# Attention values with the lower tile's keys first for all head pairs, as one accumulation per bank

## Chip, cores, metric

The kernel runs on one core of a Trainium2 chip. The metric is the device time of one execution in microseconds (us); times below are of that kind, or spans and stretches of one profiled execution. TensorE is called PE, its weight loads PEld, VectorE DVE, ScalarE ACT, GpSimd POOL, and SyncE, which issues nearly all transfers, SP.

## What is computed

Eight batches of eight heads, 576 positions, head width 64, all in float32. Attention is causal with a window of 128 keys and a linear bias by distance; its output, with the heads side by side, goes through a soft mixture of eight experts with four slots each.

```python
def _attn_ref(q, k, v):
    scores = scale * np.matmul(q, k.transpose(0, 1, 3, 2))
    ...
    mask = (rel >= 0) & (rel < window)          # window = 128
    scores = np.where(mask, scores + bias[None], -1000000000.0)
    ...
    return np.matmul(attn, v)

def _moe_ref(x, phi, w1, w2):                   # x: 4608 x 512
    logits = x @ phi                            # 32 slots
    ...                                         # d: softmax over tokens, c: softmax over slots
    slot_input = d.T @ x
    ...                                         # per expert: relu(slot_input @ w1) @ w2
    return c @ slot_out
```

## The kernel before

**Tiles and groups.** Each batch is cut into query tiles of 128 positions, t = 0 to 3, and a tail t = 4 of 64. Because the window is 128 keys, a query of tile t sees keys of its own tile up to itself, and keys of the lower tile t - 1 from itself on. A tile of t < 4 is worked in two groups, g = 0 and 1, of four heads each; a tail is one group of eight heads. There are 72 groups, and they pass through a software pipeline: the loop from line 773 on runs one group per step, and all engines execute their instructions in the order in which the program issues them.

**One step i of the loop.** DVE merges the scores of group i (`merge`, L279 to L283), takes row maxima (L301) and the bias (L304), and normalises the probabilities of group i - 1 (`normalise`, L317), with the reciprocal of a sum (L313) that POOL prepares (`total`, L309). PE turns the probabilities of group i - 3 (`flip`, L372) into the PSUM tile `pq`. ACT copies them to SBUF as `pa` (`split`, L379). Then PE computes the values of group i - 4 (`values`, L406), the scores of group i + 1 (L247, L252, L259, L266), and what else is due: `x_flip` (L434), `logits` (L452), `slot_sum` (L510). ACT ends the step with the four exponentials of group i (`expo`, L357); ahead of them it stores a finished query tile out of PSUM (`x_store`, L422) and keeps a flipped one (`x_keep`, L443). (For the first steps the lags are one less.)

**Two masked halves.** Scores of a group hold, in 128 columns, own-tile keys and lower-tile keys merged by a triangle, so the flipped probabilities must be split again. `split` does it on POOL with two triangular selects, in this order: L381 reads `pa` and writes the lower tile's part to another buffer, `pp`; L383 then masks `pa` in place for the own tile's part (`pd`). For a tail these are L386 and L388. For t = 0 there is no lower tile and no select.

**Values.** For head pair i of the group and for each half of the keys (`ph` 0: lower tile, from `pp`; `ph` 1: own tile, from `pd`), two matmuls with 64 columns of `v` as weights write 64 partitions each of the PSUM tile `xp`. One float32 matmul is two PE instructions (and two weight loads) in the profile. So a group with t of 1 to 3 has 2 pairs x 2 halves x 2 = 8 matmuls, 16 instructions; a tail 16 matmuls of 64 columns, 32 instructions; t = 0 has 4 matmuls. The order is pair by pair: lower, own, lower, own.

**Around it.** V tiles lie in three SBUF buffers; after the last group of a tile SP loads the next one (`load_v`, L191), and at the start of the last batch two tiles by halves (`load_v_pair`, L201). After the loop the last groups are unrolled by hand; there `split` and `values` of the last tail are cut in two (lines 812 to 835). From about 225 us on come the experts (L926, L963) and the combination (L988, L990).

Of the kernel before, what the change touches and what calls it, by code (L numbers as in the profile page):

```python
# [56 lines left out]
def width(t):  # L57
    return P if t < 4 else TAIL
# [10 lines left out]
def tile_attn_softmoe(  # L69
# [71 lines left out]
    st = {}  # L141
# [18 lines left out]
    number = {key: i for i, key in enumerate(groups)}  # L160
# [231 lines left out]
    def values(key, pairs=None, to=None):  # L392
        b, t, g = key
        w = width(t)
        if (b, t) not in st or to is not None:
            st[b, t] = ps_1.tile([P, NPAIR, P], F32, tag="xp", name="xp") if to is None else to
        xp = st[b, t]
        pd, pp = st[key]["pd"], st[key]["pp"]
        for i in pairs or range(2 if t < 4 else 4):
            j = 2 * g + i  # L400
            halves_of = (1,) if t == 0 else (0, 1)
            for ph in halves_of:
                for par in range(2):
                    h = 2 * j + par
                    src = pp if ph == 0 else pd
                    nc.tensor.matmul(  # L406
                        xp[D * par:D * par + D, j, 0:w], lhsT=v_slot[b, t - 1 + ph][:, D * h:D * h + D],
                        rhs=src[:, 2 * par + i] if t < 4 else src[:, 2 * par + i % 2, TAIL * (i // 2):TAIL * (i // 2) + TAIL],
                        start=(ph == halves_of[0]), stop=(ph == halves_of[-1]),
                    )  # L410

    def x_of(b, t):
# [357 lines left out]
    with tc.manual_schedule(engines=ORDERED):  # L770
        scores(0)
        loads(0)
        for i in range(n):
            new = groups[i]
            run("pre", i)
            if i:
                softmax_front(new, groups[i - 1])
            else:
                for us in (LO, HI):
                    merge(new, us)  # L780
                    rowmax(new, us)
                    bias(new, us)
                    expo(new, us)
            near = int(i < SKIP)
            if i + near >= FLAG and i != SKIP:
                flip(groups[i + near - FLAG])
                split(groups[i + near - FLAG])
            run("act", i)
            if i + near >= LAG and i != SKIP:
                values(groups[i + near - LAG])  # L790
                after_values(i, groups[i + near - LAG])
            if i + 1 < n:
                scores(i + 1)
            if i + 1 < n - 1:
                loads(i + 1)
            if i:
                expo(new)
            run("pe", i)
            load_weights_at(i)
            run("dve", i)  # L800
# [14 lines left out]
        slot_flip(end)  # L815
        token_max(end)
        values(ga)
        load_weight()
        load_weight()
# [7 lines left out]
        inverse(gd, LO)  # L827
        normalise(gd, LO)
        values(gb, range(0, 2), bank("xq"))
        flip(gd, LO, bank("pt"))  # L830
        split(gd, LO)
# [287 lines left out]
```

## Time and profile before

| | us |
|---|---|
| median of 3 runs | 291.06 (290.58 to 291.56) |
| the profiled execution's own time | 291.42 |
| its span, first to last instruction | 289.4 |

| engine | busy us | share of the span |
|---|---|---|
| PE | 256.3 | 89% |
| DVE | 222.4 | 77% |
| ACT | 206.2 | 71% |
| PEld | 179.0 | 62% |
| POOL | 112.3 | 39% |

The attention stage takes about the first 225 us of the span; experts and combination the rest. Between 25 and 200 us PE, DVE and ACT are each busy for some nine tenths of most stretches, so the shares over the whole span understate DVE and ACT there. "Idle before" in a row is the time that the engine stood still ahead of that instruction, with the instruction that ended the wait.

### The profile page before, as it was taken

The page shows a single profiled execution, that of the slowest core. Times are in us where ns is not written, and L with a number is a line of the kernel's source. Part 1 is how long each engine was busy: PE and PEld are TensorE (multiplying, and loading weights), DVE is VectorE, ACT ScalarE, POOL GpSimd, SP SyncE. Part 2 cuts the span into 40 slices and gives each one's busy share as a digit, 9 for nine tenths or more (in the row PEclk, how much of TensorE's full clock was granted, in tenths as well). Part 3 has the DMA queues.
Part 4 walks back from the last instruction along what each step waited for, and adds up shares of the span by engine and source line. Part 5 has one row for each costly group of instructions (what it writes and reads, how often), then busy time and mean ns, then how long its engine had stood idle before and what let it go on. Part 6 is the DMA issues. An engine that isn't in the chain of part 4 may idle for free.

```text
span 289.4 us, 13589 instructions
## 1 busy us (share of the span) xinstructions
PE 256.3 (89%) x5535; PEld 179.0 (62%) x5535; DVE 222.4 (77%) x509; ACT 206.2 (71%) x817; POOL 112.3 (39%) x218
## 2 busy tenths in 40 slices
PE   7598899789969989999998997998979989999990
PEld 3366666666657567766676764766666543587650
DVE  3889989898995989898898997799874344646442
ACT  2788888988885998997998898798784311044460
POOL 2044626662573267246617634466652012000000
PEclk9779999999998999999999999999999999999996
DMA  6646267868883998789678977877465579999897
GB/s 183 228 117 179 82 206 253 269 189 295 266 268 106 303 299 261 209 301 285 202 247 276 321 248 221 275 237 231 150 219 166 162 258 353 411 409 340 335 385 291
DMA packets 36754, 72.61 MB, mean 251 GB/s; under 512 B 4402, under 2 KB 15316, under 8 KB 36692
## 3 DMA queue, kind: packets, MB, share of 16 engines
q1 hardware_dynamic: 35972, 71.24, 74.5%
q8 instruction: 43, 0.70, 1.0%
q10 hardware_dynamic: 720, 0.51, 0.5%
q14 instruction: 19, 0.16, 0.2%
HBM read 62.29 MB, written 9.44 MB: 248 GB/s over the span
## 4 chain that ended last, share of the span: by engine, by line
PE 40%; ACT 18%; DVE 18%; POOL 13%; issue 6%; DMA 2%; DVEq 0%; ACTq 0%; POOLq 0%
ACT area L357 10%; PE xp L406 6%; PE op L963 5%; PE hp L926 5%; DVE area L317 5%; DVE s L301 4%; PE s L266 4%; POOL area L383 4%; POOL area L381 4%; PE po L988 3%; DVE s L281 3%; ACT area L379 3%; ACT area L422 2%; PE lp L452 2%; PE pq L372 2%
## 5 line engine op out<-in xcount | busy, mean ns | idle before, releaser
L357 ACT ACTIVATE area<-s,nb 128x128 f32<-128x128 f32 x286 | 103.1, 394 | 12.3 <-DVE nb L304 10.3
L406 PE MATMUL xp<-area 128*64 128x128 f32 (+1 forms) x1104 | 76.9, 274 | 12.1 <-POOL area L383 5.8
L406 PEld LDWEIGHTS xp<-area 128*64 128x64 f32 x1104 | 54.6, 138 | 23.3 <-POOL area L383 11.0
L357 ACT ACTIVATION_READ_ACCUMULATOR area<-s,nb 128x1 f32 x286 | 66.1, 231 | 0.0
L317 DVE TENSOR_TENSOR area<-area,rs 128x512 f32<-128x512 f32 (+1 forms) x73 | 61.6, 844 | 1.8
L379 ACT COPY area<-pq 128x512 f32<-128x512 f32 (+1 forms) x72 | 43.8, 610 | 14.5 <-PE pq L372 11.9
L301 DVE TENSOR_REDUCE s<-s 128x4 f32<-128x512 f32 x71 | 49.5, 697 | 2.2
L266 PE MATMUL s<-kq 64*32 64x160 f32 x1792 | 43.6, 306 | 1.1 <-issue 1.1
L383 POOL TENSOR_SCALAR_AFFINE_SELECT area<-area 128x512 f32<-128x512 f32 x48 | 42.4, 884 | 3.3
L309 POOL TENSOR_SCALAR rs<-sm 128x4 f32<-128x4 f32 x70 | 15.0, 214 | 73.9 <-ACT area L357 72.5
L381 POOL TENSOR_SCALAR_AFFINE_SELECT area<-area 128x512 f32<-128x512 f32 x48 | 34.5, 719 | 16.4 <-ACT area L379 14.8
L281 DVE COPY_PREDICATED s<-cst,s 128x512 f32<-128x512 int32 x48 | 33.1, 689 | 6.9 <-PE s L266 6.7
L372 PE MATMUL pq<-unit_r,area 64*128 64x64 f32 x552 | 31.4, 232 | 3.1 <-ACT area L322 2.6
L266 PEld LDWEIGHTS s<-kq 64*32 64x32 f32 x1792 | 30.1, 108 | 2.6 <-issue 1.9
L372 PEld LDWEIGHTS pq<-unit_r,area 64*128 64x128 f32 x552 | 23.4, 140 | 11.6 <-POOL rs L309 2.9
L259 PE MATMUL s<-ramp,ones 64*32 64x320 bf16 x448 | 18.9, 314 | 4.0 <-ACT area L357 3.6
L422 ACT COPY area<-xp 128x512 f32<-128x512 f32 (+1 forms) x37 | 21.2, 572 | 1.4 <-PE xp L406 0.8
L443 ACT COPY area<-pq 128x512 f32<-128x512 f32 x34 | 20.8, 612 | 0.3 <-PE pq L428 0.3
L434 PEld LDWEIGHTS pq<-unit_r,area 64*128 64x128 f32 x264 | 11.1, 140 | 13.0 <-issue 9.2
L990 ACT COPY ob<-po 128x512 f32<-128x512 f32 x19 | 10.4, 591 | 11.4 <-PE po L988 9.9
L313 DVE RECIPROCAL rs<-rs 128x4 f32<-128x4 f32 (+1 forms) x73 | 12.3, 169 | 5.1 <-POOL rs L309 4.4
L990 DVE COPY ob<-po 128x512 f32<-128x512 f32 x17 | 11.2, 687 | 6.6 <-PE po L988 5.8
(173 smaller groups left out, 329.8 us busy)
## 6 DMA issues: line engine op xcount, KB each, us to landing
w<-w SPq DMA_DIRECT2D x53, 512.0 KB, 5.5
out<-ob SPq DMA_DIRECT2D x36, 256.0 KB, 3.2
kq<-q_t SPq DMA_DIRECT2D x69, 128.0 KB, 3.4
kq<-k_t SPq DMA_DIRECT2D x32, 256.0 KB, 3.8
area<-v_n SPq DMA_DIRECT2D x31, 256.0 KB, 4.0
area<-w SPq DMA_DIRECT2D x8, 512.0 KB, 4.6
area<-v_n SPq DMA_DIRECT2D x12, 128.0 KB, 4.3
kq<-w SPq DMA_DIRECT2D x3, 512.0 KB, 6.0
```

Of the source, the lines that this page charges most:

```text
L266: nc.tensor.matmul(s4[32 * c:32 * c + 32, 2 * par + jj, 32 * r:32 * r + WIN], lhsT=qt[rows, 2 * h + jj if t == 4 else jj, 32 * r:32 * r + 32],
L281: nc.vector.copy_predicated(s4[:, :, P:2 * P], bc(mask_u, 1, 4), s4[:, :, 0:P])
L301: nc.vector.tensor_reduce(st[key]["mx"][:, us], merged(key, us), axis=AX.X, op=ALU.max, negate=True)
L317: nc.vector.tensor_tensor(p4, p4, bc(rs, 2, P), op=ALU.mult)
L357: nc.scalar.activation(s["p4"][:, u], merged(key, u), AF.Exp, bias=s["nb"][:, u:u + 1], scale=SCALE, accum_out=s["sm"][:, u:u + 1],)
L372: nc.tensor.transpose(s["pt"][:, u, r], s["p4"][rows, u], ident[rows, rows])
L379: nc.scalar.copy(pa[:, us].rearrange("p u (r w) -> p u r w", r=2), s["pt"][:, us])
L381: nc.gpsimd.affine_select(pp[:, us], pa[:, us], [[0, m], [-1, P]], ALU.is_gt, 0.0, base=0, channel_multiplier=1)
L383: nc.gpsimd.affine_select(pa[:, us], pa[:, us], [[0, m], [1, P]], ALU.is_ge, 0.0, base=0, channel_multiplier=-1)
L406: nc.tensor.matmul(xp[D * par:D * par + D, j, 0:w], lhsT=v_slot[b, t - 1 + ph][:, D * h:D * h + D], rhs=src[:, 2 * par + i] if t < 4 else ...
L422: eng.copy(dst, src[:, :, 0:w])
L990: copy_by[by](ob, po)
```

## The change

For each group the two loops change places: all head pairs take the lower tile's keys first (`ph` 0), then all take their own (`ph` 1). With t of 1 to 3 the 16 instructions of a group now read `pp` in the first 8 and `pd` in the last 8; in the order before, instructions 1 to 4 and 9 to 12 read `pp`, 5 to 8 and 13 to 16 `pd`. In a tail it is the first 16 of 32; before, the two took turns every 4. Since several pairs are now open in one PSUM bank at once, the start flag is set on the first matmul of each 64-partition half of the bank alone, for the whole query tile, and the stop flag on the last. The matmuls, their number and operands, and all other instructions are the same.

```diff
-        for i in pairs or range(2 if t < 4 else 4):
-            j = 2 * g + i
-            halves_of = (1,) if t == 0 else (0, 1)
-            for ph in halves_of:
+        parts = (1,) if t == 0 else (0, 1)
+        fresh = number[key] == 0 or st.get("bank", None) is not xp
+        st["bank"] = xp
+        done = (g == 1 or t == 4 or to is not None) and (pairs is None or pairs[-1] == 3)
+        inner = pairs or range(2 if t < 4 else 4)
+        for ph in parts:
+            for i in inner:
+                j = 2 * g + i
                 for par in range(2):
                     h = 2 * j + par
                     src = pp if ph == 0 else pd
                     nc.tensor.matmul(
                         xp[D * par:D * par + D, j, 0:w], lhsT=v_slot[b, t - 1 + ph][:, D * h:D * h + D],
                         rhs=src[:, 2 * par + i] if t < 4 else src[:, 2 * par + i % 2, TAIL * (i // 2):TAIL * (i // 2) + TAIL],
-                        start=(ph == halves_of[0]), stop=(ph == halves_of[-1]),
+                        start=(fresh and (ph, i) == (parts[0], inner[0])), stop=(done and (ph, i) == (parts[-1], inner[-1])),
                     )
```

## The prediction, made before the changed kernel ran

> **What bounds the kernel now.** I read four views: the stretches of the attention stage first, then the page's chain, the waits grouped by who ended them, and the timeline around one group; after that the chain in order of time.
>
> ```profile
> 25.00:200.00 175.00, 160.56 (x4023) 117.32 (x4025) 157.62 (x348) 152.80 (x639) 89.52 (x167) 0.99 0.77 243
> ```
>
> The columns are start and end, length, and the busy time of PE, PEld, DVE, ACT and POOL, then PE's clock. In these 175 us PE is busy 160.6, DVE 157.6, ACT 152.8: three engines at 92, 90 and 87%. No single one is the bound, and PE has 14.4 us of standing still that could be won at most here.
>
> ```profile
> span 289.4 us, 13589 instructions
> ...
> ACT area L357 10%; PE xp L406 6%; PE op L963 5%; PE hp L926 5%; DVE area L317 5%; DVE s L301 4%; PE s L266 4%; POOL area L383 4%; POOL area L381 4%; PE po L988 3%; DVE s L281 3%; ACT area L379 3%; ACT area L422 2%; PE lp L452 2%; PE pq L372 2%
> ```
>
> The chain that ended last runs through all four engines; the values (L406, 6%) and the two POOL selects that feed them (4% each) are on it.
>
> ```profile
> PEld xp L406 <- POOL area L383: 11.0, 22, 0.8
> PEld xp L406 <- POOL area L381: 5.5, 6, 1.3
> ACT area L379 <- PE pq L372: 11.9, 15, 3.0
> DVE s L281 <- PE s L266: 6.7, 12, 1.4
> SPq L191 <- PE xp L406: 35.9, 26, 4.5
> ```
>
> Columns: total us, times, longest. PE's weight loads stood still 22 times, 11.0 us together, for the second select. Downstream, ACT stood still 15 times for PE's flip and DVE 12 times for PE's scores: there a later PE is a later kernel.
>
> ```profile
> 103.60 0.97 POOL L383 TENSOR_SCALAR_AFFINE_SELECT area<-area 128x512 f32<-128x512 f32 x1
> 103.84 0.20 PEld L406 LDWEIGHTS xp<-area 128*64 128x64 f32 x4
> 104.62 0.63 PEld L406 LDWEIGHTS xp<-area 128*64 128x64 f32 x12 [0.59 <-POOL area L383]
> ...
> 37.53 0.90 PEld L406 LDWEIGHTS xp<-area 128*64 128x64 f32 x28 [0.50 <-POOL area L388]
> ...
> 63.96 0.90 PEld L406 LDWEIGHTS xp<-area 128*64 128x64 f32 x28 [0.21 <-POOL area L388]
> ```
>
> One such group: four instructions of lower-tile keys run at 103.84, PE stops for the select that ends at 104.57, and twelve are left behind it. In a tail 28 of 32 are left behind L388.
>
> **The change, part by part.** *The order.* After it, eight instructions stand ahead of the stop and eight behind it (a tail: 16 and 16). The stop's end is set by POOL and does not move; what moves is four instructions of 0.63/12 = 0.053 us, so 0.21 us, from behind the stop to ahead of it (a tail: 12 x 0.90/28 = 0.39 us). The mean stop, 11.0/22 = 0.50 us, exceeds 0.21, so four more fit in nearly always. Where PE does not stop, nothing changes. Over all 22 stops that is at most 4.6 us of PE's standing still; what counts is the part on the chain.
>
> *The flags.* Fewer start flags and the same instructions. A group of t = 0 overwrites throughout, one of t = 1 to 3 accumulates in half of its instructions:
>
> ```profile
> 61.33 0.85 PEld L406 LDWEIGHTS xp<-area 128*64 128x64 f32 x16
> ...
> 67.52 0.42 PEld L406 LDWEIGHTS xp<-area 128*64 128x64 f32 x8
> ```
>
> 0.053 us each in both, so I put overwriting against accumulating at 0, from both sides.
>
> *Waits and buffers.* No wait is added. Own-tile V is needed four instructions later, lower-tile V and `pp` come free four earlier. SP's 26 waits for a V buffer end up to 0.2 us sooner; the loads of q behind them wait for PE's scores in any case, so I count nothing, except for one place below. What hides it is the loads' lead over the values; if that were gone, it would show as a gain.
>
> *On the chain.* All pieces of it from 34 us on in which values follow a select or wait for V (the one ahead of them, at 29.5, frees only ACT's store of a tile, and I count 0):
>
> ```profile
> 34.84 0.90 PE xp L406 x12
> 37.54 1.04 PE xp L406 x28
> 46.21 0.88 PE xp L406 x12
> 63.96 1.03 PE xp L406 x28
> 85.59 1.28 PE xp L406 x12
> 107.84 0.88 PE xp L406 x12
> 112.51 0.88 PE xp L406 x12
> 133.29 0.88 PE xp L406 x12
> 153.54 0.88 PE xp L406 x12
> 167.18 0.68 PE xp L406 x8
> 179.99 0.88 PE xp L406 x12
> 189.00 0.88 PE xp L406 x12
> 197.00 0.69 PE xp L406 x13
> 202.33 0.88 PE xp L406 x12
> ```
>
> and, from the timeline, the half tail near the end of the stage:
>
> ```profile
> 219.90 0.56 PE L406 MATMUL pq<-area 128*64 128x64 f32 x10 [0.15 <-POOL area L388]
> ```
>
> Three of them need a second look:
>
> ```profile
> 35.08 0.60 ACT L379 COPY area<-pq 128x512 f32<-128x512 f32 x1
> ...
> 108.38 0.93 DVE L317 TENSOR_TENSOR area<-area,rs 128x512 f32<-128x512 f32 x1
> ...
> 167.16 0.66 ACT L379 COPY area<-pq 128x512 f32<-128x512 f32 x1
> ```
>
> After 34.84 and 167.18 the chain goes on to a select at 35.75 and 167.90; but the copy that it reads ended at 35.68 and 167.82, so ACT released it, not PE: 0 for both. After 107.84 PE's scores free DVE at 109.43, but DVE was normalising until 109.31: at most 0.12.
>
> The sum: seven plain groups (46.21, 112.51, 133.29, 153.54, 179.99, 189.00, 202.33) x 0.21 = 1.47; 85.59 at a lower clock, 0.21 x 1.28/0.88 = 0.31; the tails at 37.54 and 63.96, 0.39 and, capped by the stop, 0.21; the half tail at 219.90, where 10 behind the stop become 6, 4 x 0.032 = 0.13; 107.84, 0.12. At 197.00 the chain waits for a V load whose buffer comes free after 12 instructions of a tail, in the new order after 8: 4 x 0.032 = 0.13. Together 1.47 + 0.31 + 0.39 + 0.21 + 0.13 + 0.12 + 0.13 = 2.76 us.
>
> That is the upper end. ACT's mean stall for PE, 11.9/15 = 0.79 us, exceeds 0.21 and 0.39, so at the next engine nearly all arrives. Further on it can die where another path is as late: with DVE at 90% such a path is never far, and the lower end is 0. I take two thirds, 1.8 us, nearer the upper end because of the 0.79.
>
> The experts' part follows the attention stage on PE and moves forward with it. The profiled execution took 291.42, 2.0 more than its span and 0.36 more than the median of 291.06; from the median, 291.06 - 1.84 = **289.2 us**, and for a profile like the one shown 289.6.
>
> **The rivals.** *Swallowed (no change).* The order works but the next path takes over at most places; under 0.87 us (0.3%, about what a measurement of this kernel can tell from no change) is left: some 290.7. For it speaks the even load of PE, DVE and ACT; against it the stalls of 11.9 and 6.7 us that PE causes. That the order does not do what it says, because the stop would stand ahead of the first instruction, is out: four instructions run ahead of it now.
>
> *A clock dip goes (larger gain).*
>
> ```profile
> 83.00:86.00 3.00, 1.23 (x22) 0.85 (x18) 2.85 (x7) 2.12 (x10) 2.73 (x5) 0.99 0.81 255
> 86.00:88.50 2.50, 2.50 (x54) 1.49 (x52) 1.04 (x4) 1.51 (x8) 1.68 (x3) 0.50 0.56 205
> 88.50:91.00 2.50, 2.50 (x58) 2.08 (x58) 2.23 (x5) 0.34 (x1) 0.00 (x0) 0.83 0.19 54
> ```
>
> After 3 us with PE busy for 1.23, its clock fell to 0.50 and 0.83 for 5 us in which it never stood still: 2.5 x 0.50 + 2.5 x 0.17 = 1.7 us lost. The new order fills 0.2 us of just that gap. If the dip goes, 289.2 - 1.7 = 287.5. A second dip elsewhere would cost as much and leave 290.9, which I count with no change. The Trainium skill ("TensorE: Matmul & The Clock Gate", section "Why this matters for your kernels") asks for idle gaps of more than about 3 us before the clock drops. By that rule no dip would come or go and the sum would stay; the trace disagrees, since the longest wait in the group of first-select stops is 1.3 us and the clock fell to 0.50 nonetheless.
>
> *Normalising runs into the selects (slower).*
>
> ```profile
> L317 DVE TENSOR_TENSOR area<-area,rs x73: 415/850/1154, 9.6 to 218.3; 128x512 f32<-128x512 f32 x70, 128x256 f32<-128x256 f32 x3
> ```
>
> L317 has the same work in nearly every group and takes from 0.69 (99.55) to 1.13 us (102.94, below) by whether a select runs beside it.
>
> ```profile
> 99.55 0.69 DVE L317 TENSOR_TENSOR area<-area,rs 128x512 f32<-128x512 f32 x1
> 102.94 1.13 DVE L317 TENSOR_TENSOR area<-area,rs 128x512 f32<-128x512 f32 x1
> ```
>
> A PE that is earlier brings flips, copies and selects forward against DVE. Each further hit costs 0.44 us on an engine that is 90% busy. From 1.8/0.44, so 5, more hits on the gain is gone, from (1.8 + 0.87)/0.44, so 7, the kernel is slower; nine give 289.2 + 4.0 = 293.2. For it: DVE pieces of L317 are on the chain, and the median of 0.85 leaves many groups that are not yet hit. Against it: a shift of 0.2 us is small beside a select, and may as well part the two. The Trainium skill ("SBUF — State Buffer", section "Who interferes with whom") says that a VectorE instruction with two SBUF inputs contends with a GpSimd instruction that reads SBUF, and that issue order decides who blocks; this trace's 0.69 and 1.13 agree with the first half.
>
> **How the numbers follow.** Forecast (a gain of 0.9 to 2.8, so 288.3 to 290.2 on its own) 0.50; the dip goes 0.12; swallowed, or a second dip, 0.23; normalising hit 0.15. Faster by over 0.3% takes the first two, 0.62; within 0.3% 0.23; slower 0.15. The range leaves out the far part of the dip case, 0.06, and about two thirds of the slow case, 0.10: 287.5 to 292.2.
>
> **What would show it.** Values in runs of eight (a tail 16) ahead of the stop and eight behind it; the loads' wait for L383 down from 11.0 us to about 22 x (0.50 - 0.21) = 6.4; as many instructions and the same 0.053 us each; ACT's stalls for the flip shorter; L317's mean still near its 0.85. It is wrong if L317's median rises to 1.0 or more, if dips of the clock come in other places, or if the waits for L383 shrink and the waits for a bias on ACT, or for ACT's copies on POOL, grow by as much.

## The result, and the profile after

| | us |
|---|---|
| kernel before, median of 13 runs beside the changed one | 292.82 (290.58 to 295.81) |
| changed kernel, median of 13 runs | 288.87 (287.23 to 293.67) |
| ratio, with its 95% interval | 0.9883 (0.9846 to 0.9919) |
| spans of the two profiled executions | 289.4 before, 286.0 after |

The change makes the kernel faster by 1.2% (0.8 to 1.5%): 3.4 us of the 291.06 that the prediction started from (2.4 to 4.5), so 287.7 on that footing, against a forecast of 289.2. Some runs of any kernel fall into a slower state with a lower granted clock; the medians above hold all runs, the ratios and their intervals only those outside that state, and the ratios carry the verdicts.

The waits grouped by who ended them, of the changed kernel (values are line L410 now; columns: total us, times, longest):

```profile
ACT area L379 <- PE pq L372: 9.0, 15, 1.3
PEld xp L410 <- POOL area L381: 6.1, 6, 1.5
DVE s L281 <- PE s L266: 5.6, 8, 1.4
PEld xp L410 <- POOL area L383: 5.4, 15, 0.6
```

The stop for the second select fell from 11.0 us in 22 waits to 5.4 us in 15; the stop for the first select did not fall (5.5 to 6.1). Downstream, ACT's wait for PE's flip fell from 11.9 to 9.0 us and DVE's for PE's scores from 6.7 to 5.6.

One such group in the timeline after:

```profile
44.76 0.97 POOL L383 TENSOR_SCALAR_AFFINE_SELECT area<-area 128x512 f32<-128x512 f32 x1
45.07 0.42 PEld L410 LDWEIGHTS xp<-area 128*64 128x64 f32 x8
45.78 0.42 PEld L410 LDWEIGHTS xp<-area 128*64 128x64 f32 x8 [0.29 <-POOL area L383]
```

Eight loads now run ahead of the stop and eight behind it, each still 0.42/8 = 0.053 us. The stop is what is left of the select.

The stretches of the attention stage and the chain by lines, after:

```profile
25.00:200.00 175.00, 161.24 (x4085) 118.87 (x4091) 159.88 (x354) 155.43 (x653) 93.03 (x171) 1.00 0.79 247
```

```profile
ACT area L357 9%; PE xp L410 7%; DVE area L317 6%; DVE s L301 6%; PE s L266 5%; PE op L967 5%; PE hp L930 5%; PE po L992 4%; DVE s L281 3%; POOL area L381 3%; PE pq L372 3%; PE lp L456 2%; DVE s L279 2%; PE s L259 2%; ACT area L379 2%
```

All of PE, DVE and ACT do more in the same 175 us (DVE 157.6 to 159.9, ACT 152.8 to 155.4; PE 160.6 to 161.2, though the 160.6 holds some 1.7 us that the clock dip of that execution added): the pipeline as a whole moves faster. L383, 4% of the chain before, is no longer among its first fifteen lines; L381 is.

Where the time came from, by pieces of the chain that stand for the same work (the logits of some passes, and the experts' first hidden layer), before and then after:

```profile
39.77 1.01 PE lp L452 x32
66.19 1.01 PE lp L452 x32
114.58 1.01 PE lp L452 x32
182.06 1.01 PE lp L452 x32
234.87 7.07 PE hp L926 x64
```

```profile
39.35 1.01 PE lp L456 x32
65.02 1.01 PE lp L456 x32
111.48 1.01 PE lp L456 x32
178.32 1.01 PE lp L456 x32
231.17 7.07 PE hp L930 x64
```

The lead grows 0.42, 1.17, 3.10, 3.74 and stands at 3.70 at the experts, whose own part is nearly unchanged (289.4 - 234.87 = 54.5 before, 54.8 after). Some gain is made in every part of the attention stage. But 1.9 of the 3.7 us is made between 66 and 115 us, where the execution before had its clock dip (86 to 91 us) and the one after had none there; so this pair of profiles does not tell the gain of the order from that of the dip, and the runs below have to.

### The profile page after: what moved, and what is told of

It reads as the page before. It is cut to its first block, busy times and chain, and to the rows that moved or that the text cites. A ratio compares the mean times of both kernels' runs of the same rounds, so it can differ in the third digit from the quotient of the medians.

```text
span 286.0 us, 13588 instructions
## 1 busy us (share of the span) xinstructions
PE 253.9 (89%) x5535; PEld 178.9 (63%) x5535; DVE 221.6 (77%) x509; ACT 205.6 (72%) x817; POOL 112.9 (39%) x218
## 4 chain that ended last, share of the span: by engine, by line
PE 45%; DVE 23%; ACT 16%; POOL 7%; issue 5%; DMA 2%; DVEq 0%; ACTq 0%; POOLq 0%
ACT area L357 9%; PE xp L410 7%; DVE area L317 6%; DVE s L301 6%; PE s L266 5%; PE op L967 5%; PE hp L930 5%; PE po L992 4%; DVE s L281 3%; POOL area L381 3%; PE pq L372 3%; PE lp L456 2%; DVE s L279 2%; PE s L259 2%; ACT area L379 2%
## 5 line engine op out<-in xcount | busy, mean ns | idle before, releaser
L410 PE MATMUL xp<-area 128*64 128x128 f32 (+1 forms) x1104 | 74.5, 272 | 8.4 <-POOL area L381 5.3
L357 ACT ACTIVATION_READ_ACCUMULATOR area<-s,nb 128x1 f32 x286 | 65.4, 229 | 0.0
L410 PEld LDWEIGHTS xp<-area 128*64 128x64 f32 x1104 | 54.1, 137 | 18.0 <-POOL area L381 6.1
L383 POOL TENSOR_SCALAR_AFFINE_SELECT area<-area 128x512 f32<-128x512 f32 x48 | 41.7, 870 | 3.3
L381 POOL TENSOR_SCALAR_AFFINE_SELECT area<-area 128x512 f32<-128x512 f32 x48 | 35.5, 740 | 15.5 <-ACT area L379 14.6
L372 PE MATMUL pq<-unit_r,area 64*128 64x64 f32 x552 | 31.3, 233 | 3.7 <-ACT area L322 2.8
L438 PE MATMUL pq<-unit_r,area 64*128 64x64 f32 x264 | 15.2, 233 | 0.9 <-ACT area L379 0.6
```

What stands on the lines that cost most here:

```text
L357: nc.scalar.activation(s["p4"][:, u], merged(key, u), AF.Exp, bias=s["nb"][:, u:u + 1], scale=SCALE, accum_out=s["sm"][:, u:u + 1],)
L372: nc.tensor.transpose(s["pt"][:, u, r], s["p4"][rows, u], ident[rows, rows])
L381: nc.gpsimd.affine_select(pp[:, us], pa[:, us], [[0, m], [-1, P]], ALU.is_gt, 0.0, base=0, channel_multiplier=1)
L383: nc.gpsimd.affine_select(pa[:, us], pa[:, us], [[0, m], [1, P]], ALU.is_ge, 0.0, base=0, channel_multiplier=-1)
L410: nc.tensor.matmul(xp[D * par:D * par + D, j, 0:w], lhsT=v_slot[b, t - 1 + ph][:, D * h:D * h + D], rhs=src[:, 2 * par + i] if t < 4 else ...
L438: nc.tensor.transpose(xq[:, j, r], x[rows, j], ident[rows, rows])
```

## Experiments

Theory A, that of the prediction: the order acts through PE's stop for the second select and nothing else. Rivals: B, that the clock dip of the first profile went; C, that the fewer start flags are faster; D, that the new order is better for PE by itself. Kernels of one series ran beside the same runs of the kernel before. In the diffs, lines are cut to the core.

**The changed kernel again, and clocks.** No edit.

> The changed kernel once more, beside the others of this series. Theory A (stops for the second select): the loads' wait for L383 again near 5.4 us against 11.0 before, and a ratio of 0.985 to 0.992 to the kernel before. Theory B (the clock dip of the profile before is what went): the ratio lies near 1 wherever the mean clocks of the runs agree, and the difference follows the clock alone.

Measured: 0.9881 (0.9840 to 0.9922). Its profile has no dip of the clock in the attention stage, a span of 287.1 us, and these stops:

```profile
PEld xp L410 <- POOL area L381: 6.4, 6, 1.5
PEld xp L410 <- POOL area L383: 5.7, 17, 0.6
```

Each run lists its mean granted clock. A line fitted through the 22 runs of the kernel before that count for the ratio in this series falls by 1.4 us for each 0.01 of clock and passes 291.8 us at a clock of 0.98; a line through the nine such runs of the changed kernel passes 288.6 there. At one clock the difference is 3.2 us, so rival B, which wanted none, falls. The clock explains part of the scatter and little of the difference.

**The flags alone.**

```diff
-        for ph in parts:
-            for i in inner:
+        for ph, i in [(ph, i) for i in inner for ph in parts]:   # order of before, flags of after
```

> The old order, lower and own keys by turns, with the new flags: one start per bank and half, one stop. Theory A: no change, ratio 0.997 to 1.003, PE stops for L383 as before, 11 us in the loads. Rival C (the fewer start flags are what is faster): ratio near 0.988, as for the whole change.

Measured: 1.0041 (1.0002 to 1.0080), with stops like before and no clock dip in its profile, which still spans 288.8 us, against 286.0 and 287.1 in the two profiles of the changed kernel, which have none between 25 and 225 us either:

```profile
PEld xp L410 <- POOL area L383: 10.0, 20, 0.8
PEld xp L410 <- POOL area L381: 5.4, 6, 1.3
```

Rival C falls. But 1.0041 lies outside the 0.997 to 1.003 that was expected, so the flags were measured once more, with the kernel before itself as a control in the same series.

> The kernel before as a control, treated like a changed one: ratio 1 within 0.4%. What it is off by is the scatter that every other ratio of these series may carry. If it comes out at 1.004 like the flags alone, the flags cost nothing.

> The flags alone once more. Theory A: no cost, ratio as the control's within 0.4%. Rival E (an accumulating write or the longer accumulation costs some 0.4%, and the order alone would have given more than the whole change): 1.003 to 1.008 with the control at 1.

Measured: the control 0.9988 (0.9951 to 1.0026), the flags 0.9965 (0.9912 to 1.0018). Rival E, a cost of the flags, finds no support: in two series they came out on either side of 1. A ratio may be off by about 0.4% here, and a cost below that is not excluded.

**The halves the other way round.**

```diff
-        parts = (1,) if t == 0 else (0, 1)
+        parts = (1,) if t == 0 else (1, 0)
```

> The new nesting with the halves the other way round: own keys first for all pairs, then the lower tile's. All 16 instructions of a group (a tail: all 32) now stand behind the second select, where it was 12 (28) before and 8 (16) after. Theory A: the price is a straight line in this number, so about as much slower than before as the change is faster, ratio 1.008 to 1.018, with the loads' wait for L383 at 15 to 20 us. Theory B: ratio near 1 at equal clock. Rival C: 0.988, since the flags are the new ones.

Measured: 1.0126 (1.0081 to 1.0172).

```profile
PEld xp L410 <- POOL area L383: 22.2, 27, 2.3
ACT area L379 <- PE pq L372: 16.6, 18, 2.1
DVE s L281 <- PE s L266: 9.9, 13, 2.5
```

With 16, 12 and 8 instructions of a full tile's group behind the second select the ratio is 1.013, 1 and 0.988: a straight line within the intervals, and both its ends have the same flags and instructions. ACT's wait for the flip goes 16.6, 11.9, 9.0 us. The stop came out longer than the 15 to 20 us expected. The stops for the first select (5.5 us before) seem to be in it: no wait of the values for L381 is left in this profile, since PE waits once, for the later of the two; and 11.0 x 16/12 + 5.5 = 20.2.

**One part alone.**

```diff
+        pairwise = [(ph, i) for i in inner for ph in parts]
-        for ph in parts:
-            for i in inner:
+        for ph, i in pairwise if t < 4 else [(ph, i) for ph in parts for i in inner]:   # tails only; body only: t == 4
```

> The new order in the eight tails alone; the tiles of 128 queries keep the old order, all with the new flags. Theory A by the sum of the prediction: the tails' terms are 0.39 + 0.21 + 0.13 + 0.13 = 0.86 of 2.76 us, so a third of the gain, ratio 0.995 to 0.999. If the tails carried most of it: 0.99 or less.

> The new order in the tiles of 128 queries, the old one in the tails, with the new flags. Theory A: nearly all of the gain, ratio 0.986 to 0.993, since the tails alone gave none that could be measured. If the two parts only work together: 0.995 or more.

Measured: tails 1.0009 (0.9965 to 1.0053), body 0.9934 (0.9899 to 0.9970).

```profile
PEld xp L411 <- POOL area L383: 10.1, 20, 0.8
PEld xp L411 <- POOL area L381: 4.6, 5, 1.3
```

```profile
PEld xp L411 <- POOL area L381: 6.3, 6, 1.5
PEld xp L411 <- POOL area L383: 5.3, 15, 0.6
```

In the tails-only kernel (first fence) the stops for the second select stay, in the body-only kernel (second fence) they are as short as with the whole change. The body's share is 0.0066 of 0.0117; 0.9934 misses the expected 0.986 to 0.993 by 0.0004. For the tails the 0.6 us that the prediction gave them (0.86/2.76 of 1.8, a ratio of 0.998) lies inside the interval, and so does nothing: the run is inconclusive there. Added up the two parts give 0.0057, half of the whole. By the intervals the missing 0.006 may be scatter (about 0.007 for such a sum); whether the parts need each other stays open.

**Without the second select, in both orders.** The own-tile part of the probabilities stays unmasked.

```diff
-            nc.gpsimd.affine_select(
-                pa[:, us], pa[:, us], [[0, m], [1, P]], ALU.is_ge, 0.0, base=0, channel_multiplier=-1)
```

and the same for the tails' second select.

> The kernel before without the second select (L383 and L388): the own-tile part of the probabilities is left unmasked, so this part of the computation is left out. No values wait for a second select any more. Theory A: faster than the changed kernel, ratio 0.96 to 0.985 (11.0 us of stops gone, and 42 us of work on POOL that slows DVE's normalising).

> The changed kernel without the second select; the own-tile part is left unmasked here too. Theory A (the order acts through the stop for this select alone): the same time as the old order without it, within 0.4%. Rival D (the new order is better for PE by itself, or by earlier free buffers): still about 1.2% ahead of it.

Measured: the old order 0.9657 (0.9594 to 0.9721), the new one 0.9681 (0.9614 to 0.9747); spans 282.0 and 281.6 us. With the select gone, so is the difference between the orders: the new one is 0.25% behind, give or take 0.9%, where rival D wanted it 1.2% ahead. D falls as the whole cause, and what only A says has come out; a part of the gain that does not go through the select is excluded only above some 0.7%.

**The other stop: a multiplication ahead of the selects.** The six stops for the first select that the change left alone have one cause. POOL and PE in the changed kernel at one of them:

```profile
55.89 0.40 POOL L549 TENSOR_TENSOR ln<-ln,cs 128x128 f32<-128x128 f32 x1 [0.91 <-DVE rs L313]
56.24 1.09 POOL L381 TENSOR_SCALAR_AFFINE_SELECT area<-area 128x512 f32<-128x512 f32 x1
57.39 0.42 PEld L410 LDWEIGHTS xp<-area 128*64 128x64 f32 x8 [1.52 <-POOL area L381]
```

and in the grouped waits:

```profile
POOL ln L549 <- DVE rs L313: 5.6, 7, 1.3
```

In these rows POOL runs the multiplication of the slot weights (L549) ahead of the select; it waits 0.91 us for DVE (5.6 us in seven waits; six of the seven stand right ahead of the six stops), and the first select waits behind it, though the copy that it reads ended at 54.78. The multiplication's own operand is the reciprocal of L548, which ends at 55.81; the profile names L313, the next one, which ends 0.06 us later. The select also takes 1.09 us here, with DVE normalising beside it, and 0.63 us at the same step of the kernel below. Nobody reads the product before the experts.

```diff
-            lambda: mul(slots(k), slots(k), bc(cs[:, 0:m], 2, NS), op=ALU.mult),
+            (lambda: post.append(scale_up)) if k < end else scale_up,
 ...
                 split(groups[i + near - FLAG])
+            after_split()          # issues what is in post
```

> The changed kernel with one POOL instruction moved: the multiplication of the slot weights (L549, L545 before), which stands ahead of both selects in six steps and waits there for DVE, is issued behind them. The stops that are left for the first select (6 of them, 6.1 us in the loads, right behind that multiplication) should go. Theory A (a stop of the values on the chain is worth most of its length): 2 to 4 us less than the changed kernel, ratio to the kernel before 0.975 to 0.981. If DVE's chain is as late in these steps: no more than 0.5 us, ratio 0.986 to 0.99.

Measured: 0.9750 (0.9682 to 0.9818), a median of 284.11 us, span 280.1 us: the fastest version that computes the reference.

```profile
PEld xp L414 <- POOL area L387: 5.4, 16, 0.6
PEld xp L414 <- POOL area L385: 1.2, 1, 1.2
```

```profile
25.00:200.00 175.00, 166.04 (x4157) 122.72 (x4158) 161.94 (x364) 158.59 (x667) 95.71 (x176) 1.00 0.80 250
```

(L385 and L387 are the two selects here.) The stops for the first select fall from 6.1 to 1.2 us, and PE is busy for 166.0 of 175 us. Part of the gain may be the shorter select: L381's 48 executions took 35.5 us in all, at their new place, as L385, 32.3.

> The slot weights' multiplication behind the selects, in the old order of the values. If the stops for the two selects add up: the same gain of about 1.3% as on the changed kernel, ratio 0.983 to 0.99. If the two fixes lie on one chain and cover each other: nearly all of after_late_mul's gain, 0.975 to 0.98. If the multiplication's stop is only paid because the new order comes first: 0.995 or more.

Measured: 0.9812 (0.9755 to 0.9869), with 8.9 us of stops for the second select and 0.2 for the first:

```profile
PEld xp L410 <- POOL area L387: 8.9, 20, 0.8
PEld xp L410 <- POOL area L385: 0.2, 1, 0.2
```

The multiplication alone gives 1.9%, the order alone 1.2%, both 2.5%. The 0.9812 lies between the two ranges expected (0.983 to 0.99 if the stops add up, 0.975 to 0.98 if they cover each other). Added up the two gains would be 3.1%, which is inside the interval of both together (1.8 to 3.2%); whether they overlap a little stays open.

**All kernels by their stops.** Both selects' waits in the weight loads, summed from the fences above, against the ratio:

| kernel | stops, us | ratio |
|---|---|---|
| own keys first | 22.2 | 1.0126 |
| before | 11.0 + 5.5 = 16.5 | 1 |
| flags alone | 10.0 + 5.4 = 15.4 | 1.0041, 0.9965 |
| tails only | 10.1 + 4.6 = 14.7 | 1.0009 |
| changed | 5.4 + 6.1 = 11.5 | 0.9883, 0.9881 |
| body only | 5.3 + 6.3 = 11.6 | 0.9934 |
| before, late multiplication | 8.9 + 0.2 = 9.1 | 0.9812 |
| changed, late multiplication | 5.4 + 1.2 = 6.6 | 0.9750 |

From first to last row 15.6 us of stops are worth 0.0376 x 291.06 = 10.9 us, 0.70 us for each us. The line is rough: it passes 0.9945 for tails only and 0.987 for body only, both below their intervals, and 0.996 for the flags alone, below the first interval. The stops of one kernel also differ between profiles: the second ones give 10.5 + 7.0 = 17.5 us before, 10.5 + 5.5 = 16.0 for the flags and 5.7 + 6.4 = 12.1 changed. The two kernels without the second select, with 6.1 and 5.6 us of stops for the first, lie 0.5 to 0.8% below the line: there some 42 us of work on POOL went as well.

These are the stops of the weight loads. PE's own rows, of its matmuls, show shorter ones (L406 before, L410 changed):

```profile
PE xp L406 <- POOL area L383: 5.8, 18, 0.6
PE xp L406 <- POOL area L381: 4.7, 6, 1.2
PE xp L410 <- POOL area L383: 1.3, 4, 0.4
PE xp L410 <- POOL area L381: 5.3, 6, 1.4
```

The two rows sum to 10.5 us before and 6.6 changed; with the 18.4 us of own keys first and the 2.4 us of the last row of the table, one us of these is worth 10.9/16.0 = 0.68 us.

## Why the prediction was right

*The order.* As predicted: eight ahead, eight behind, 0.053 us each, and no cost for accumulating (the two runs of the flags alone). The loads' stop for L383 was forecast to fall to 6.4 us and fell to 5.4, with seven of the 22 waits gone (5.7 in 17 waits in the second profile). Four loads at each of 22 stops take up 4.6 us at most; 5.6 went, and what took the rest is not shown. In PE's own rows 5.8 - 1.3 = 4.5 us went.

*What the gain is worth.* The forecast was 1.8 us, two thirds of a sum of 2.76; measured are 3.4 (2.4 to 4.5). So the mechanism was right and the size was low: 1.8 lies outside the interval, while the whole sum of 2.76 lies inside it. That the time falls into the range is in part luck. From the starting median it is 287.7 us (286.6 to 288.7), and the forecast's own 288.3 to 290.2 does not hold the 287.7; the range does, because it was stretched to 287.5 for the dip, and at one clock the gain was still there.

Two readings of the low size are left. Either nearly all of the stops on the chain came through, and taking two thirds of them was the error. Or the sum was too small, because it left out all stops off the chain that ended last: of all the loads' stops 16.5 - 11.5 = 5.0 us went, and 0.70 x 5.0 = 3.5. With three engines nearly equally loaded the chain of one execution may be one sample of many near-equal ones. But by PE's own rows it is 0.68 x (10.5 - 6.6) = 2.7, no more than the chain's sum. No run tests single stops off the chain, and the interval of 2.4 to 4.5 us holds both readings, so this stays open.

*The tails.* At the tail that the prediction priced at 0.39, the loads' stop went from 0.50 to 0.19, so 0.31:

```profile
36.42 0.99 POOL L388 TENSOR_SCALAR_AFFINE_SELECT area<-area 128x512 f32<-128x512 f32 x1
36.70 0.58 PEld L410 LDWEIGHTS xp<-area 128*64 128x64 f32 x16 [0.21 <-issue]
37.47 0.55 PEld L410 LDWEIGHTS xp<-area 128*64 128x64 f32 x16 [0.19 <-POOL area L388]
```

*The rivals.* Swallowed: no, the next engines moved too. The dip: in the first pair of profiles it did go, where the clock had been 0.50 before:

```profile
83.00:86.00 3.00, 2.08 (x58) 1.41 (x58) 2.84 (x5) 2.00 (x10) 2.71 (x5) 1.00 0.81 264
86.00:88.50 2.50, 2.50 (x70) 2.17 (x64) 2.32 (x6) 1.21 (x6) 0.75 (x2) 1.00 0.33 102
```

But it had gone from the first flags-only profile as well, and that kernel is no faster than before:

```profile
83.00:86.00 3.00, 1.24 (x24) 0.86 (x22) 2.92 (x7) 2.44 (x10) 2.48 (x4) 1.00 0.98 315
86.00:88.50 2.50, 2.50 (x84) 2.00 (x88) 2.00 (x6) 1.50 (x8) 1.92 (x4) 1.00 0.54 184
```

PE is busy for 1.24 us of the first 3 here, as it was for 1.23 before the dip, with the same two waits of 1.17 and 0.60 us, and the clock stays at 1.00. In the second flags-only profile it falls in the same place, and in the second profile of the kernel before at 60 us instead. So a dip belongs to an execution more than to the kernel, and the gap that the prediction named does not bring it by itself. Normalising under the selects: no, its duration did not rise.

```profile
L317 DVE TENSOR_TENSOR area<-area,rs x73: 413/841/1149, 10.0 to 214.7; 128x512 f32<-128x512 f32 x70, 128x256 f32<-128x256 f32 x3
```

The median is 0.841 us against 0.850. The prediction's reading of this row needs a correction. Its example without a select, 0.69 us at 99.55, had a select beside it too:

```profile
99.83 0.90 POOL L381 TENSOR_SCALAR_AFFINE_SELECT area<-area 128x512 f32<-128x512 f32 x1 [0.60 <-ACT area L379]
102.89 0.64 POOL L381 TENSOR_SCALAR_AFFINE_SELECT area<-area 128x512 f32<-128x512 f32 x1 [0.27 <-ACT area L379]
```

At 99.55 normalising began first and took 0.69 us, the select 0.90; at 102.94 the select had begun 0.05 us earlier and took 0.64 us, normalising 1.13. So in these two which of them begins first decided which of them was slowed.

## What to carry to other kernels

When an engine waits in the middle of a group for the second of two products, put all work that needs only the first ahead of the wait; here keeping the accumulations open cost nothing that could be measured, and a us of stop removed was worth some 0.7 us over these kernels. Look then at what the remaining stops share: a cheap instruction on an in-order engine that waits for another engine ahead of a critical one (here 0.40 us of work in six steps) was worth at least as much as the reordering, 1.9% (1.3 to 2.5) against 1.2% (0.8 to 1.5).

## What was not expected of the hardware

In the series of the first flags-only run the mean granted clock of the kernel before went from 0.967 to 0.992 between the runs that count, and the time with it, 293.3 to 289.7 us; comparing two single runs would have credited or charged the change with that. The size is not a constant of the kernel: the line that falls by 1.4 us for each 0.01 there falls by 0.1 and 0.8 us in the two other series. And many sums open in one PSUM bank, started by one flag for each 64-partition half, cost nothing measurable: the flags alone gave 1.0041 and 0.9965 against a control of 0.9988, and without the second select the two orders gave 0.9681 and 0.9657.
